# Column sums by TensorE for the weights' scales, and products with the values three ticks behind the scores, in an attention, Fourier and feed-forward kernel

## The chip, the cores and the metric

The kernel runs on one core of one Trainium2 chip. The metric is the device time of one execution in microseconds (us), taken as the median of several executions. Of the kernel before there are three: 1055.57, 1049.64 and 1053.56 us, so the median is 1053.56 us. One more execution was taken with the hardware profiler; it took 1049.91 us.

## The reference

```
q, k, v: (4, 8, 768, 64) float32; centroids: (8, 16, 64); w_ch1: (512, 2048); w_ch2: (2048, 512)

q_assign = argmax(q_n . c_n)            # every query and key goes to one of 16 clusters
k_assign = argmax(k_n . c_n)
mask = q_assign[:, :, :, None] == k_assign[:, :, None, :]
scores = where(mask, q @ k.T / 8, -1e9)
attn = softmax(scores)
x = (attn @ v), heads side by side      # (4, 768, 512)

u = x + real(fft over the sequence of fft over the channels of x)
un = (u - mean) / sqrt(var + 1e-6)
out = u + relu(un @ w_ch1) @ w_ch2
```

## The kernel before

**Numbers in two halves.** Nearly every float32 operand is split into a high and a low float16 part, scaled by a power of two, and a product is three matmuls (high x high, high x low, low x high). Such splits are made by ScalarE (high part) and by VectorE or GpSimd (the rest).

**Attention.** The four sequences have four pairs of heads each, so there are 16 pairs, `pr`. A pair has six row tiles of 128 queries, `st`. One tile is one *tick*: `Attention.scores` (L309) makes the scores of both heads j in PSUM (L320, the mask's product L325), VectorE scales them and takes the extreme of each row in one instruction (L339, output `ju`, row value `m`), ScalarE takes the exponential (L343 in the first sequence, L345 later) and casts it to float16 (L353), GpSimd takes the rest (L354), and a DMA on SyncE's queue transposes both halves into a buffer `pt` (L356). `pt` has `PT` = 5 buffers. `Attention.attend` (L363) multiplies the transposed weights with the values (L374 to L376) into `ps_o`, of which there is one; after every third tile `finish` (L386 to L390, VectorE) divides by the sums and writes X. In the first sequence `ju` is a part of X[1], which is free by then, and the exponential reads it from there, with scale -1; in the later ones `ju` is a bfloat16 scratch tile that nobody reads, and the exponential reads the scores in PSUM with the scale from a column `e`. `prep` brings in a pair: loads, row maxima (L216, L248), scales (L225 to L227), splits (L235, L236), the assignment to clusters (L263 to L303); `split_v` (L199 to L201) splits the values into one of four buffers.

**Weights.** `Weights.run` (L546) brings in the two weight matrices as 32 blocks k of 128 x 512, in steps that lie beside the first sequence's ticks (about 1.46 steps a tick, from the first tick on). float32 values arrive as four 16-bit words each. `largest` (L486) takes the largest absolute value of each row of a block (L491, VectorE) three steps ahead; `signs` (L514) turns the top words into positive and negative parts, two ScalarE instructions a block (L519, L520) one step ahead; `join` (L523) puts them together by two matmuls (L528) and an OR by VectorE (L532); `halve` (L534), one step later, makes the float16 parts with the scale (ScalarE L538, L541, then VectorE L544 or GpSimd L542). The scale is one power of two for each four blocks g of w_ch1, got over the partitions by a matmul and a reduce (`block`, L498, with L48 and L504), and one for each row of w_ch2. `top_power` (L55) makes it by four small VectorE instructions (L58 to L61), on one column for w_ch1 and on four for w_ch2. At the end `relative` (L571) makes the factors that the feed-forward part uses.

**Fourier and feed-forward.** `Fourier.fold` (L647) folds a finished sequence in two and transposes it, `transform` does the DFT by matmuls, `FeedForward.up` (L845) and `down` (L870) are the two products with the weights. They belong to sequence b and run while the attention of sequence b+1 does; those of the last sequence run alone at the end.

**Order of the work.** `Overlap.run` (L981) gives every piece a tick and an order inside it: scores of tick t first (order 1), then the products with the values of tick t - `LAG` (order 3, LAG = 2), splits of values (4.5), weights' steps last (6). TensorE runs its instructions in exactly this order. On the other engines a planner orders them by its own estimate of the times, and each engine then runs its list in order, waiting for semaphores; so does SyncE, which issues all the DMAs. PSUM is 3 buffers `ps_f` of a bank, 2 of `ps_big` for the scores, and the one `ps_o`.

Of the kernel before, what the change touches and what calls it, by code (L numbers as in the profile page):

```python
# [25 lines left out]
P = 128  # L26
# [28 lines left out]
def top_power(nc, tops, s, inv):  # L55

    t = tops.bitcast(I32)
    nc.vector.tensor_scalar(out=t, in0=t, scalar1=20, scalar2=None, op0=ALU.logical_shift_right)  # L58
    nc.vector.tensor_scalar(out=t, in0=t, scalar1=-910.0, scalar2=1.0, op0=ALU.add, op1=ALU.max)
    nc.vector.tensor_scalar(out=inv.bitcast(I32), in0=t, scalar1=240.0, scalar2=float(1 << 23), op0=ALU.min, op1=ALU.mult)  # L60
    nc.vector.reciprocal(out=s, in_=inv)  # L61
# [20 lines left out]
class Attention:  # L82
# [226 lines left out]
    def scores(self, pr, st):  # L309
        nc, sb = self.nc, self.sb  # L310
        assert self.ready >= pr
        (hq, hk), oh, (e, ne) = self.hl[pr], self.oht[pr], self.sc.scores(pr)
# [14 lines left out]
        for j in range(2):  # L327

            m = sb.tile([P, 1], F32, name="rmx", tag="rmx", bufs=6)
            early = pr < H // 2  # L330
            if early:

                n = (2 * st + j) % self.RING * S
                p32 = self.X[1].rearrange("p a x -> p (a x)")[:, n:n + S]
            else:
                p32 = sb.tile([P, S], F32, name="p32", tag="p32", bufs=2)
            x = p32.rearrange("p (h x) -> p h x", h=2)
            ju = x if early else sb.tile([P, 2, SH], BF16, name="ju", tag="ju")
            self.mark = nc.vector.tensor_scalar(out=ju, in0=ps[j][:, :, 0:SH], scalar1=ne, scalar2=None, op0=ALU.mult, op1=ALU.min,  # L339
                                    accum_out=m)  # L340
            self.late = m
            if early:
                nc.scalar.activation(p32, p32, AF.Exp, bias=m, scale=-1.0)  # L343
            else:
                nc.scalar.activation(x, ps[j][:, :, 0:SH], AF.Exp, bias=m, scale=e)  # L345
# [8 lines left out]
            nc.gpsimd.tensor_tensor(out=ph[:, 1], in0=p32, in1=ph[:, 0], op=ALU.subtract)  # L354
# [79 lines left out]
class Weights:  # L434
# [7 lines left out]
    RAW, PN = tuple(4128 * i for i in range(6)) + (29696, 33824), (24768, 26816)  # L442
    ID, TOP, MX = 28864, 29376, 29472
    X32 = 37952, 40000
    EXTRA, A2, AHEAD = 0, 9, 7

    def __init__(self, tc, pool, arena, psf, w1, w2, ident):
# [6 lines left out]
        self.inv = [pool.tile([P, n], F32, name=f"winv{n}") for n in (4, 16)]  # L454
# [31 lines left out]
    def largest(self, k):  # L486

        nc, at = self.nc, self.arena.at
        g, i = divmod(k, 4)
        mx = at(self.MX + 32 * (g % 2), [P, 4], F32)  # L490
        nc.vector.tensor_reduce(out=mx[:, i:i + 1], in_=self.top(k).bitcast(BF16), op=ALU.max, axis=AX.X,  # L491
                                apply_absolute_value=True)
        if i == 3 and g >= 4:
            self.scales(g, mx)
        elif i == 3:
            nc.vector.tensor_reduce(out=mx[:, 0:1], in_=mx, op=ALU.max, axis=AX.X)

    def block(self, g):  # L498

        nc, at = self.nc, self.arena.at  # L500
        mx = at(self.MX + 32 * (g % 2), [P, 4], F32)
        ps = self.psf()
        along(nc, ps[:, 0:P], mx[:, 0:1], self.ident)
        nc.vector.tensor_reduce(out=mx[:, 1:2], in_=ps[:, 0:P], op=ALU.max, axis=AX.X)  # L504
        self.scales(g, mx[:, 1:2])

    def scales(self, g, mx):
        n = mx.shape[1]
        s = self.sb.tile([P, 4], F32, name="wsc", tag="wsc", bufs=2)
        top_power(self.nc, mx, s[:, 0:n], self.inv[0][:, g:g + 1] if n == 1 else self.inv[1][:, 4 * (g - 4):4 * (g - 3)])  # L510
        for i in range(4):
            self.scale[4 * g + i] = s[:, i % n:i % n + 1]

    def signs(self, k):  # L514

        nc, at = self.nc, self.arena.at
        pn = at(self.PN[k % 2], [P, 2, DM], BF16)
        top = self.top(k)
        nc.scalar.activation(pn[:, 0].bitcast(I16), top.bitcast(I16), AF.Relu, bias=self.off[:, 0:1], scale=8.0)  # L519
        nc.scalar.activation(pn[:, 1].bitcast(I16), top, AF.Relu, bias=self.off[:, 1:2], scale=8.0)  # L520
        self.bits[k] = pn
# [12 lines left out]
    def halve(self, k):  # L534
# [4 lines left out]
        if k % 2:  # L539
            x = self.arena.at(self.X32[k // 2 % 2], [P, DM], F32)  # L540
# [5 lines left out]
    def run(self):  # L546
# [5 lines left out]
        for i in range(2):  # L552
            nc.gpsimd.tensor_scalar(out=self.idb[:, i], in0=self.ident, scalar1=1.0 - 2 * i, scalar2=None, op0=ALU.mult)
        for k in range(-self.AHEAD, 33):
# [16 lines left out]
    def relative(self):  # L571

        nc, at = self.nc, self.arena.at
        top, m1, r = (at(self.TOP + 32 * j, [P, 1], F32) for j in range(3))
        rel = self.rel
        nc.vector.tensor_tensor(out=rel.rearrange("p (a c) -> p a c", c=4),
                                in0=self.inv[1].rearrange("p (a c) -> p a c", c=4),
                                in1=self.inv[0].rearrange("p (a o) -> p a o", o=1).broadcast_to([P, 4, 4]), op=ALU.mult)
        nc.vector.tensor_reduce(out=m1, in_=rel, op=ALU.max, axis=AX.X)
        ps = self.psf()  # L580
        along(nc, ps[:, 0:P], m1, self.ident)
        nc.vector.tensor_reduce(out=top, in_=ps[:, 0:P], op=ALU.max, axis=AX.X)
        nc.vector.reciprocal(out=r, in_=top)
        nc.vector.tensor_scalar(out=rel, in0=rel, scalar1=r[:, 0:1], scalar2=HSC, op0=ALU.mult, op1=ALU.mult)
# [36 lines left out]
class Fourier:  # L621
# [25 lines left out]
    def fold(self, b):  # L647
# [5 lines left out]
        mid = at(self.XM, [1, M + 1], F32)  # L653
        nc.gpsimd.tensor_copy(out=mid, in_=X[0:1, 3, 0:M + 1])
        nc.gpsimd.tensor_tensor(out=mid[:, 1:M], in0=mid[:, 1:M], in1=X[0:1, 3, DM - 1:M:-1], op=ALU.add)
        last = at(self.XL, [P, 3], F32)
        xt = {}
        for i, op in self.FOLDS:
# [9 lines left out]
            xt[i] = t.rearrange("p (a t c) x -> p a t c x", a=2, t=3)  # L668
        self.parts[b] = xt, last, mid, s
# [119 lines left out]
HSC = float(2.0 ** -20)  # L789


class FeedForward:


    NT = 2 * P
# [49 lines left out]
    def up(self, blk):  # L845
# [6 lines left out]
        for f in range(16):  # L852
# [9 lines left out]
            if f % 2:  # L862
                nc.vector.tensor_scalar(out=r, in0=ps, scalar1=rel[:, f:f + 1], scalar2=0.0, op0=ALU.mult, op1=ALU.max)  # L863
            else:
                nc.scalar.activation(r, ps, AF.Relu, scale=rel[:, f:f + 1])
            nc.scalar.activation(hh[:, f], ps, AF.Relu, scale=rel[:, f:f + 1])  # L866
# [31 lines left out]
PT = 5  # L898


class Overlap:
# [23 lines left out]
    PIN, PF, PV = (), 29, 1  # L925
    CE, WP, WQ = 0.45, 0, 0
# [54 lines left out]
    def run(self):  # L981
# [43 lines left out]
        for pr in range(NP):  # L1025
# [36 lines left out]
def cluster_attention_fourier_ffn_kernel(ctx, tc, q, k, v, cent, w1, w2, cd, sd, cm, cs, ss, ny, out):  # L1062
# [6 lines left out]
    arena = Arena(glob, 47264)  # L1069
# [47 lines left out]
```

## Time and profile before

| | |
|---|---|
| median of three executions | 1053.56 us (1049.64 to 1055.57) |
| profiled execution | 1049.91 us |
| its span, first to last instruction | 1048.1 us |
| busy: TensorE, VectorE, ScalarE, GpSimd | 910.8, 627.4, 625.3, 586.9 us |
| share of 16 DMA engines, hardware queue | 65.9% |

In the profile PE is TensorE's matmuls, PEld its weight loads, DVE VectorE, ACT ScalarE, POOL GpSimd, SP and SPq SyncE and its queue. A row of a group has line, engine, operation, output and inputs with shapes, the count after the x, then the busy time in us and the mean duration of one in ns, then the idle time of the engine just before and what ended it. A row of waits has who waited for whom, the total in us, how often, and the longest. A row of a window has its bounds, its length, the busy time of each engine with its instructions in brackets, TensorE's granted clock as a share of full speed, the mean busy share of the 16 DMA engines and GB/s. By the start of VectorE's L339 the first sequence's ticks run from 31 to 208 us, those of the second from 208 to 419, of the third from 419 to 643, and of the fourth to 862.

### The profile page before, as it was taken

How to read it: one execution, taken by the hardware profiler on the slowest of the kernel's cores; microseconds unless marked ns; L12 is line 12 of the kernel's file. 1: busy time of each engine (PE TensorE's matmuls, PEld its weight loads, DVE VectorE, ACT ScalarE, POOL GpSimd, SP SyncE). 2: the span in 40 equal slices, each digit the busy share in tenths (PEclk: the TensorE clock that was granted, in tenths of full speed). 3: DMA queues.
4: the chain of work that ended last, by engine and by line, in shares of the span. 5: the costliest groups of instructions: out<-in, count | busy, mean ns of one | idle time of the engine just before them, and what ended most of it. 6: DMA issues, size and time to landing. Idle time of an engine off the chain costs nothing.

```text
span 1048.1 us, 23542 instructions
## 1 busy us (share of the span) xinstructions
PE 910.8 (87%) x9350; PEld 591.7 (56%) x9362; DVE 627.4 (60%) x1297; ACT 625.3 (60%) x980; POOL 586.9 (56%) x693
## 2 busy tenths in 40 slices
PE   3665565749899999998899999997999999999998
PEld 2333333425575756655666757555757667576674
DVE  8789899767757555668656555667555333631110
ACT  4798889755766665645666746556756543351230
POOL 2364565753975756655856646647847645271230
PEclk9987878769899999999899999998999999999999
DMA  7799998979887776568877767588757562321000
GB/s 272 179 225 245 196 239 166 171 156 153 177 123 153 128 154 121 121 137 161 153 137 142 140 128 132 110 141 170 124 102 133 96 110 43 81 52 31 11 11 21
DMA packets 396239, 140.01 MB, mean 134 GB/s; under 512 B 381784, under 2 KB 381792, under 8 KB 396128
## 3 DMA queue, kind: packets, MB, share of 16 engines
q1 hardware_dynamic: 396128, 138.50, 65.9%
q8 instruction: 73, 1.20, 0.5%
q14 instruction: 38, 0.31, 0.1%
HBM read 42.52 MB, written 6.29 MB: 47 GB/s over the span
## 4 chain that ended last, share of the span: by engine, by line
PE 39%; DVE 6%; DMA 3%; ACT 3%; POOL 2%; issue 2%; SPq 0%; ACTq 0%; DVEq 0%; POOLq 0%
PE ps_f L888 16%; PE ps_f L858 13%; PE ps_big L320 3%; DMA pt<-ph 3%; PE ps_f L713 2%; DVE ju L339 1%; ACT p L345 1%; PE ps_o L374 1%; POOL ph L354 1%; PE ps_o L375 1%; PE ps_o L376 1%; PE ps_big L325 1%; ACT ph L353 1%; DMA scr<-in_k_dram 0%; DVE arena L660 0%
## 5 line engine op out<-in xcount | busy, mean ns | idle before, releaser
L354 POOL TENSOR_TENSOR ph<-p,ph 128x768 f16<-128x768 f32 x144 | 242.9, 1688 | 184.6 <-ACT ph L353 150.1
L858 PE MATMUL ps_f<-arena,w1h 128*128 128x256 f16 x1536 | 271.4, 277 | 19.1 <-ACT arena L866 9.0
L888 PE MATMUL ps_f<-w2h,arena 128*128 128x512 f16 x768 | 238.9, 379 | 0.0
L345 ACT ACTIVATE p<-ps_big,rmx,sce 128x768 f32<-128x768 f32 x144 | 142.1, 988 | 132.9 <-DVE ju L339 127.5
L858 PE MATMUL ps_f<-arena,w1l 128*128 128x256 f16 x768 | 212.4, 277 | 0.0
L339 DVE TENSOR_SCALAR_CACHE_REDUCE ju<-ps_big,sce 128x768 bf16<-128x768 f32 x144 | 146.1, 1014 | 68.2 <-PE ps_big L325 58.2
L888 PEld LDWEIGHTS <-arena 128*128 128x128 f16 x1152 | 108.7, 98 | 126.6 <-issue 5.2
L858 PEld LDWEIGHTS <-w1h 128*128 128x128 f16 x1536 | 152.1, 99 | 36.0 <-issue 14.3
L867 POOL TENSOR_TENSOR arena<-arena 128x256 f16<-128x256 f32 x192 | 128.1, 677 | 77.3 <-ACT arena L866 73.6
L320 PE MATMUL ps_big<-hlk,hlq 64*128 64x384 f16 x1152 | 128.9, 348 | 39.0 <-ACT p L345 23.4
L374 PE MATMUL ps_o<-v,pt 128*128 128x66 f16 x1152 | 124.8, 198 | 43.0 <-DVE X L390 27.5
L888 PE MATMUL ps_f<-w2l,arena 128*128 128x512 f16 x384 | 145.5, 379 | 0.0
L374 PEld LDWEIGHTS <-pt 128*128 128x128 f16 x1152 | 110.2, 100 | 57.7 <-issue 37.1
L353 ACT CAST ph<-p 128x768 f16<-128x768 f32 x144 | 119.6, 832 | 15.0 <-DMA pt<-ph 12.8
L375 PE MATMUL ps_o<-v,pt 128*128 128x64 f16 x1152 | 124.8, 199 | 0.0
L376 PE MATMUL ps_o<-v,pt 128*128 128x66 f16 x1152 | 124.5, 198 | 0.0
L866 ACT ACTIVATE arena<-ps_f,wrel 128x256 f16<-128x256 f32 x192 | 90.1, 472 | 54.8 <-DVE arena L863 54.7
L863 DVE TENSOR_SCALAR arena<-ps_f,wrel 128x256 f32<-128x256 f32 x96 | 46.3, 482 | 124.9 <-PE ps_f L858 66.4
L320 PEld LDWEIGHTS <-hlq 64*128 64x128 f16 x1152 | 55.5, 99 | 101.5 <-issue 72.7
L375 PEld LDWEIGHTS <-pt 128*128 128x128 f16 x1152 | 110.7, 101 | 2.8
L376 PEld LDWEIGHTS <-pt 128*128 128x128 f16 x1152 | 111.1, 103 | 0.0
L858 PEld LDWEIGHTS <-w1l 128*128 128x128 f16 x768 | 76.1, 99 | 20.2 <-issue 10.7
(178 smaller groups left out, 1330.4 us busy)
## 6 DMA issues: line engine op xcount, KB each, us to landing
arena<-in_moe_w_ch_dram SPq DMA_DIRECT2D x32, 512.0 KB, 6.8
scr<-in_q_dram SPq DMA_DIRECT2D x16, 384.0 KB, 2.9
scr<-in_k_dram SPq DMA_DIRECT2D x16, 384.0 KB, 4.5
vst<-in_v_dram SPq DMA_DIRECT2D x16, 384.0 KB, 3.5
out_dram<-arena SPq DMA_DIRECT2D x24, 256.0 KB, 2.3
pt<-ph SPq DMA_TRANSPOSE x168, 3.9
arena<-in_cs_dram SPq DMA_DIRECT2D x12, 192.0 KB, 3.5
arena<-in_ss_dram SPq DMA_DIRECT2D x12, 192.0 KB, 3.5
```

The source lines that it names most:

```text
L320: nc.tensor.matmul(out=ps[j][:, hf, 0:SH], lhsT=hq[rows[j], a, sl], rhs=hk[rows[j], c, hs], start=(i == 0), stop=False)
L339: self.mark = nc.vector.tensor_scalar(out=ju, in0=ps[j][:, :, 0:SH], scalar1=ne, scalar2=None, op0=ALU.mult, op1=ALU.min, accum_out=m)
L345: nc.scalar.activation(x, ps[j][:, :, 0:SH], AF.Exp, bias=m, scale=e)
L353: nc.scalar.copy(out=ph[:, 0], in_=p32)
L354: nc.gpsimd.tensor_tensor(out=ph[:, 1], in0=p32, in1=ph[:, 0], op=ALU.subtract)
L374: nc.tensor.matmul(out=o[:, at:at + W], lhsT=hi, rhs=v16[:, kt, 0:W], start=(kt == 0), stop=False)
L375: nc.tensor.matmul(out=o[:, at:at + D], lhsT=hi, rhs=v16[:, kt, 66:130], start=False, stop=False)
L376: nc.tensor.matmul(out=o[:, at:at + W], lhsT=lo, rhs=v16[:, kt, 0:W], start=False, stop=(kt == ST - 1))
L858: nc.tensor.matmul(out=ps.rearrange("p (t x) -> p t x", x=P), lhsT=a[:, dc, fs], rhs=c[:, :, dc], start=(i == 0), stop=(i == 11))
L866: nc.scalar.activation(hh[:, f], ps, AF.Relu, scale=rel[:, f:f + 1])
L867: nc.gpsimd.tensor_tensor(out=hl[:, f], in0=r, in1=hh[:, f], op=ALU.subtract)
L888: nc.tensor.matmul(out=ps, lhsT=a[:, f, ts], rhs=c[:, f], start=(i == 0), stop=(i == 47))
```

## The change

The row maxima (`largest`, L491) go. Instead the new `block` multiplies, for four blocks of weights, the positive and negative parts (`bits`) by a matrix of ones on TensorE: eight matmuls into one bank give the sums over the 128 rows for each of 512 columns, on every partition; one VectorE reduce takes the largest, and `top_power` works on that one column, for both matrices. `signs` treats two blocks in one pair of instructions, two steps ahead, into three buffers instead of two. `join` is as before, but comes after `block` in the step. In the first sequence the products with the values come three ticks after the scores, up to the 22nd tile; `pt` has six buffers in all sequences. In the later sequences `ju` lies in PSUM over the scores, and the exponential reads it there with the constant scale -1. The copies for the middle row of the Fourier part (`mid`, two small GpSimd instructions) are moved behind the two folds. `x` in `halve` has one buffer instead of two, some places and constants change with it, and `relative` needs no matmul.

```diff
-def top_power(nc, tops, s, inv):
+def top_power(nc, tops, t, s, inv):
-    t = tops.bitcast(I32)
-    nc.vector.tensor_scalar(out=t, in0=t, scalar1=20, scalar2=None, op0=ALU.logical_shift_right)
-    nc.vector.tensor_scalar(out=t, in0=t, scalar1=-910.0, scalar2=1.0, op0=ALU.add, op1=ALU.max)
+    t = t.bitcast(I32)
+    nc.vector.tensor_scalar(out=t, in0=tops.bitcast(I32), scalar1=23, scalar2=None, op0=ALU.logical_shift_right)
+    nc.vector.tensor_scalar(out=t, in0=t, scalar1=-13.0, scalar2=1.0, op0=ALU.add, op1=ALU.max)
...
-            ju = x if early else sb.tile([P, 2, SH], BF16, name="ju", tag="ju")
+            ju = x if early else ps[j][:, :, 0:SH]
...
-            if early:
-                nc.scalar.activation(p32, p32, AF.Exp, bias=m, scale=-1.0)
-            else:
-                nc.scalar.activation(x, ps[j][:, :, 0:SH], AF.Exp, bias=m, scale=e)
+            nc.scalar.activation(x, ju, AF.Exp, bias=m, scale=-1.0)
...
+    def block(self, g):
+        nc, at = self.nc, self.arena.at
+        ps = self.psf()
+        i = 0
+        for k in range(4 * g, 4 * g + 4):
+            for j in range(2):
+                nc.tensor.matmul(out=ps, lhsT=self.ones[:, 0:1].broadcast_to([P, P]), rhs=self.bits[k][:, j], start=(i == 0), stop=(i == 7))
+                i += 1
+        mx = at(self.MX + 32 * (g % 2), [P, 1], F32)
+        nc.vector.tensor_reduce(out=mx, in_=ps, op=ALU.max, axis=AX.X)
+        s = self.sb.tile([P, 1], F32, name="wsc", tag="wsc", bufs=2)
+        top_power(nc, mx, ps[:, 0:1], s, self.inv[g // 4][:, g % 4:g % 4 + 1])
+        for i in range(4):
+            self.scale[4 * g + i] = s[:, 0:1]
...
     def signs(self, k):
-        pn = at(self.PN[k % 2], [P, 2, DM], BF16)
-        top = self.top(k)
+        pn = at(self.PN[k // 2 % 3], [P, 2, 2, DM], BF16)
+        raw = at(self.RAW[k % len(self.RAW)], [P, 2, 4 * DM + 16], U16)
+        top = raw[:, :, 4:4 + 4 * DM].rearrange("p a (n f) -> p a n f", f=4)[:, :, :, 0]
         nc.scalar.activation(pn[:, 0].bitcast(I16), top.bitcast(I16), AF.Relu, bias=self.off[:, 0:1], scale=8.0)
         nc.scalar.activation(pn[:, 1].bitcast(I16), top, AF.Relu, bias=self.off[:, 1:2], scale=8.0)
-        self.bits[k] = pn
+        self.bits[k], self.bits[k + 1] = pn[:, :, 0], pn[:, :, 1]
...
         for k in range(-self.AHEAD, 33):
-            if k >= 1 and k % 4 == 1 and k < 16:
-                self.block(k // 4)
             for p in self.loads(k):
                 self.load(p)
-            if 0 <= k + 3 < 32:
-                self.largest(k + 3)
-            if 0 <= k + 1 < 32:
-                self.signs(k + 1)
+            if k % 2 == 0 and 0 <= k + 2 < 32:
+                self.signs(k + 2)
+            if k % 4 == 0 and 0 <= k < 32:
+                self.block(k // 4)
             if 0 <= k < 32:
                 self.join(k)
             if k >= 1:
                 self.halve(k - 1)
...
-PT = 5
+PT = 6
...
+    LATE = 22
...
                 at(t0 + st, 1, att.scores, pr, st)
-                at(t0 + st + self.LAG, 3, att.attend, pr, st)
+                at(t0 + st + self.LAG + (6 * pr + st < self.LATE), 3, att.attend, pr, st)
```

More of the change, by code (lines that the diff above doesn't have):

```diff
@@ L452, in __init__ @@
         self.dsc = pool.tile([P, 1], F32, name="dsc")
-        self.inv = [pool.tile([P, n], F32, name=f"winv{n}") for n in (4, 16)]
+        self.inv = [pool.tile([P, 4], F32, name=f"winv{n}") for n in range(2)]
         self.rel = pool.tile([P, 16], F32, name="wrel")
@@ L861, in up @@
             r = at(self.HR[f % 2], [P, self.NT], F32)
[L862 to L866, printed above, removed]
+            with self.tc.high_priority() if self.HP else contextlib.nullcontext():
+                if f % 2:
+                    nc.vector.tensor_scalar(out=r, in0=ps, scalar1=rel[:, f:f + 1], scalar2=0.0, op0=ALU.mult, op1=ALU.max)
+                else:
+                    nc.scalar.activation(r, ps, AF.Relu, scale=rel[:, f:f + 1])
+                nc.scalar.activation(hh[:, f], ps, AF.Relu, scale=rel[:, f:f + 1])
             nc.gpsimd.tensor_tensor(out=hl[:, f], in0=r, in1=hh[:, f], op=ALU.subtract)
```

60 lines of the change are left out of this document (20 added, 40 removed).

## The prediction

> **What bounds the kernel now.** I read the table of windows first, cut at the ticks of each sequence, because a share of the whole span would mix stages that have different limits.
>
> ```profile
> core 0: us, PE busy (x) PEld busy (x) DVE busy (x) ACT busy (x) POOL busy (x), PEclk, DMA share, GB/s
> 0.00:31.00 31.00, 12.95 (x52) 6.60 (x53) 25.04 (x72) 15.15 (x24) 5.54 (x38) 1.00 0.68 239
> 31.00:208.00 177.00, 110.58 (x1313) 65.58 (x1324) 151.08 (x311) 153.17 (x219) 105.02 (x90) 0.83 0.96 207
> 419.00:643.00 224.00, 211.56 (x2313) 139.26 (x2311) 142.73 (x287) 137.48 (x215) 139.55 (x162) 0.98 0.72 137
> 643.00:862.00 219.00, 207.22 (x2263) 136.35 (x2262) 126.20 (x255) 131.46 (x203) 134.36 (x152) 0.98 0.70 127
> ```
>
> From 419 us on TensorE is busy for 94 to 95% of the time and is the limit. In the first sequence, 31 to 208 us, it is busy for 62%; VectorE is at 85%, ScalarE at 87%, and the DMA share reads 0.96. So in the stage that the weights share with the first sequence there are three candidates, and the change works on two of them. Next I asked what ScalarE and TensorE waited for in that window.
>
> ```profile
> ACT X L343 <- DVE X L339: 7.6, 5, 2.5
> ACT w2h L538 <- DVE ps_f L532: 5.8, 6, 2.7
> ACT w1h L538 <- DVE wsc L61: 4.6, 3, 3.0
> ...
> PE ps_o L374 <- DVE X L390: 27.5, 6, 5.5
> PE ps_big L320 <- DVE X L339: 14.8, 17, 3.7
> PE ps_o L374 <- DMA pt<-p: 8.2, 7, 2.6
> PE ps_o L374 <- DMA pt<-ph: 6.8, 4, 2.2
> PE ps_f L528 <- DVE w1l L544: 4.6, 3, 2.8
> ```
>
> ScalarE is idle for 177 - 153.2 = 23.8 us, and 18.0 us of it is waiting for VectorE. TensorE waits 42.3 us for VectorE and 15.0 us for transposes that have not landed. VectorE runs late, and the others queue behind it. Last I looked at the DMA share in short windows, to see what 0.96 means.
>
> ```profile
> 78.00:80.00 2.00, 2.00 (x39) 1.31 (x39) 2.00 (x3) 2.00 (x4) 0.00 (x0) 1.00 1.00 399
> 94.00:100.00 6.00, 3.90 (x57) 2.37 (x57) 5.21 (x11) 2.83 (x5) 3.07 (x2) 0.88 1.15 204
> 121.00:122.00 1.00, 0.66 (x19) 0.66 (x20) 0.90 (x4) 0.87 (x2) 0.00 (x0) 1.00 0.00 0
> ```
>
> With loads alone, 399 GB/s, a full microsecond reads 1.00; with transposes, 204 GB/s, it reads 1.15, since packets overlap; and there are gaps of 0.00. So 0.96 over 177 us is 148 us (at 1.15) to 170 us (at 1.00) of full use. The change moves the same bytes, so this is a floor under the stage.
>
> **The scales, on VectorE.** The rows by form:
>
> ```profile
> L491 DVE TENSOR_REDUCE arena<-arena 128x1 f32<-128x512 bf16 x32 | 21.7, 680 | 8.0 <-DMA arena<-in_moe_w_ch_dram 7.9
> L504 DVE TENSOR_REDUCE arena<-ps_f 128x1 f32<-128x128 f32 x4 | 1.1, 284 | 0.6 <-PE ps_f L48 0.6
> L59 DVE TENSOR_SCALAR arena<-arena 128x4 int32<-128x4 int32 x4 | 4.6, 1143 | 0.1
> L60 DVE TENSOR_SCALAR winv<-arena 128x4 int32<-128x4 int32 x4 | 6.2, 1547 | 0.1
> L60 DVE TENSOR_SCALAR winv<-arena 128x1 int32<-128x1 int32 x4 | 0.6, 151 | 0.1
> L277 DVE TENSOR_REDUCE mx<-ps_f 128x24 f32<-128x384 f32 x16 | 8.8, 551 | 0.6 <-PE ps_f L271 0.6
> L216 DVE TENSOR_REDUCE amx<-scr 128x1 f32<-128x768 f32 x32 | 30.4, 950 | 22.4 <-DMA scr<-in_q_dram 19.4 <-DMA scr<-in_k_dram 2.8
> ```
>
> Removed: 32 row maxima, 21.7 us; four L504, 1.1; the four-column chain of w_ch2, 4.6 + 6.2 for L59 and L60 and 8 x 0.151 = 1.2 for its other two, costed as one-column ones; the one-column chain of w_ch1, 16 x 0.151 = 2.4. Together 37.2 us. Added: eight reduces of 512 columns from PSUM. The slope from L277 to L216 is (950 - 551) / 384 = 1.04 ns a column, so one costs 551 + 128 x 1.04 = 684 ns, eight 5.5 us; and 32 one-column instructions, 4.8 us. Together 10.3 us, net 26.9 us less.
>
> Not all of it lies in the stage; eight maxima run ahead of it, of which these are the first and the last:
>
> ```profile
> 9.28 0.68 DVE L491 TENSOR_REDUCE arena<-arena 128x1 f32<-128x512 bf16 x1
> ...
> 21.59 0.68 DVE L491 TENSOR_REDUCE arena<-arena 128x1 f32<-128x512 bf16 x1
> ```
>
> So the stage loses 24 x 0.68 + 15.5 = 31.8 us and gains seven eighths of 10.3, 9.0 us: VectorE there goes from 151.1 to about 128 us. Ahead of the stage VectorE is busy for 25 of 31 us, with the first pair's preparation between those maxima. But eight of the new matmuls now stand ahead of the first scores. I take 1 us off, between 3 us off (most maxima had delayed that preparation) and 3 us on (the matmuls are late).
>
> **The signs, on ScalarE, and the sums, on TensorE.**
>
> ```profile
> L519 ACT ACTIVATE arena<-arena 128x512 int16<-128x512 int16 x32 | 24.1, 753 | 4.6 <-PE ps_f L528 1.6 <-PE ps_o L376 1.5 <-DMA scr<-in_q_dram 1.5
> L520 ACT ACTIVATE arena<-arena 128x512 int16<-128x512 uint16 x32 | 24.0, 749 | 0.0
> L199 ACT ACTIVATE v<-vst,scp 128x384 f16<-128x384 f32 x32 | 18.4, 611 | 0.0
> L235 ACT ACTIVATE hlk<-scr,scp 128x768 f16<-128x768 f32 x16 | 14.7, 921 | 0.0
> L528 PE MATMUL ps_f<-arena 128*128 128x512 bf16 x52 | 22.0, 510 | 6.8 <-DVE w1l L544 4.6 <-DVE arena L58 1.0 <-issue 0.7
> ```
>
> From L199 to L235 a further element costs (921 - 611) / 384 = 0.81 ns. A sign instruction of 1024 elements is then 0.75 + 512 x 0.81 = 1.17 us; 32 of them 37.3 us in place of 48.1. I put 9.7 us of these 10.8 in the stage: ScalarE goes from 153.2 to 143.5 us. TensorE gets 64 matmuls of L528's form, 22.0 / 52 = 0.42 us each, 27 us in all: in the stage from 111 to about 135 of some 165 us. It has that room; what hides the matmuls is its present waiting.
>
> What the change adds is an order. `block` stands in TensorE's list ahead of `join` and the next scores, and it needs signs issued in the same step, where `join` had its signs a step earlier. If ScalarE is late with them, `join`, the next tick's scores, and so VectorE's L339 and ScalarE's own next exponential stand behind. Bounds: 0 if the planner places the signs early, as now, where L528 waits for VectorE and ScalarE is not in its list; and 8 x (2 x 1.17 + 8 x 0.42) = 46 us if signs and matmuls are exposed every time. I take 0.3 us a group, 2.4 us, near the lower end because of that list. The wait of L538 for the scale, 4.6 us with four groups, now comes with eight: another 4.6 us.
>
> **Sum of the stage.** ScalarE is the engine that I count by: its work 143.5, its idle time 23.8, of which I take off half of the 18.0 us of waits for VectorE, because VectorE's share falls from 85% to 128 / 165 = 78% and not to zero; and the new 2.4 + 4.6. That gives 143.5 + 23.8 - 9.0 + 7.0 = 165.3 us in place of 177, or 11.7 less. It lies in the middle of the DMA floor of 148 to 170.
>
> **Three ticks and six buffers.** These can take away the 15.0 us in which TensorE waits for transposes, or nothing: the longer wait of the same L374, 27.5 us for L390, stays, because there is still one `ps_o` and VectorE releases it. With six buffers and three ticks all six are in use when tile t is transposed, so its DMA needs the products of tile t - 3, which TensorE runs just before; if they are late, the loads behind it on SyncE's queue wait too. And the values' buffers come free a tick later:
>
> ```profile
> POOL v L200 <- PE ps_o L376: 16.5, 4, 7.1
> POOL w1l L542 <- ACT arena L541: 12.8, 5, 4.3
> ```
>
> GpSimd already stands for 16.5 us before L200, with L354 and so the transposes behind it. One tick more (177 / 24 = 7.4 us) at each of four places is 30 us of GpSimd at worst, of which it has 177 - 105 = 72 idle. Gain and loss face each other; I take 0, between 15 off and 15 on. The single buffer of `x` costs nothing, because L542 waits for ScalarE and not the other way round; the moved GpSimd copies and the shorter `relative` are costed at nothing as well, and the fold would show it if they delayed it.
>
> **`ju` in PSUM, in the later sequences.**
>
> ```profile
> L339 DVE TENSOR_SCALAR_CACHE_REDUCE ju<-ps_big,sce 128x768 bf16<-128x768 f32 x144 | 146.1, 1014 | 68.2 <-PE ps_big L325 58.2 <-ACT arena L866 2.0 <-DVE ju L339 0.9
> L227 DVE TENSOR_REDUCE ps_f<-ps_f 128x3 f32<-128x384 f32 x16 | 8.9, 559 | 15.1 <-PE ps_f L48 15.1
> L345 ACT ACTIVATE p<-ps_big,rmx,sce 128x768 f32<-128x768 f32 x144 | 142.1, 988 | 132.9 <-DVE ju L339 127.5 <-POOL ph L354 5.4
> L641 ACT ACTIVATE arena<-ps_f 128x257 f16<-128x257 f32 x24 | 9.3, 388 | 15.6 <-PE ps_f L728 9.8 <-PE ps_f L713 4.1 <-DVE arena L642 1.1
> L866 ACT ACTIVATE arena<-ps_f,wrel 128x256 f16<-128x256 f32 x192 | 90.1, 472 | 54.8 <-DVE arena L863 54.7
> PE ps_big L320 <- ACT p L345: 10.1, 8, 3.0
> ```
>
> A reduce into PSUM (L227) costs 8 ns more than one into SBUF (L277), so L339 goes to about 1022 ns. An activation from PSUM with a constant scale (L641) costs 84 ns less than one with the scale from a column (L866), so L345 goes to about 904 ns: 12.1 us less of ScalarE. It is on the path only where TensorE waits for it: after 250 us, 10.1 us in eight stretches (last row). Two exponentials a tick make 0.17 us off each, 1.3 us, and VectorE gives some of it back: 1 us off, between 12 off and 2 on.
>
> [...]
>
> **Total.** 1 + 11.7 + 0 + 1 = 13.7 us off the profiled 1049.9 gives 1036.2 us. The median of the runs lies 3.7 us above that profiled execution, so I forecast 1040 us.
>
> **Rivals.** The first is that the loop closes up. If all of ScalarE's waits for VectorE go and no new ones come, the stage is 143.5 + 5.8 = 149 us, at the lower DMA floor; with the other 2 us that is 30 off, 1024 us. For it: VectorE would be at 86% there only if nothing else slowed it. Against it: DMA would have to run without the gaps shown.
>
> The second is that DMA is already the limit, and the lag does nothing because six buffers just cover three ticks. At the upper floor of 170 us with gaps as today, the stage saves 2 us, and the total is 1050 us. For it: 0.96. Against it: the window at 0.00, and SyncE's transposes wait for GpSimd's results.
>
> The third is slower: TensorE stuck in `block`, waiting for signs that ScalarE has placed behind exponentials. If half of the 46 us is exposed, 23 us against 13.7 give 1063 us. From 1.7 us a group on it eats the gain; from 2.4 us the kernel is slower by half a per cent. For it: ScalarE is 87% busy and in order. Against it: the signs depend on loads made long before.
>
> **Chances.** A measurement of this kernel can tell about 0.5%, 5.3 us, from no change. The forecast case has 0.58, the loop closing up 0.12, DMA 0.16, the stuck list 0.14. The first two are faster, the third is about no change, the fourth slower. The range takes in the loop closing up, DMA, and the bounds of the small terms: 1024 to 1056 us.
>
> **What would show it.** In the profile after: no L491; eight reduces of 128x512 near 0.68 us; signs near 1.17 us; ticks 0 to 24 of L339 in about 165 us with VectorE near 128 and ScalarE near 143.5; L345's successor near 0.90 us; few waits of the products for `pt`. I am wrong if the first stage has not become shorter, if the column sums wait for ScalarE by more than 1.7 us a group, or if later stages move by more than 5 us.

## The result, and the profile after

The changed kernel takes 1042.51 us (median of 7 runs, 1041.02 to 1048.06); beside it the kernel before took 1051.6 us (7 runs, the three already shown among them). The ratio is 0.9914 with a 95% interval of 0.9893 to 0.9935: about 9 us faster, which is more than the 0.5% that a measurement can tell. The profiled execution after took 1042.51 us with a span of 1040.7; the one before, 1049.91, lies at the low end of its runs, so the two spans differ by only 7.4 us.

Where did those 7.4 us come from? I cut both spans at the starts of L339 in ticks 0, 24, 48, 72 and 95. A sequence has 24 ticks, so these are the prefix, the four sequences and the tail (us):

| part | before | after | difference |
|---|---|---|---|
| ahead of the first L339 | 31.1 | 28.8 | -2.3 |
| ticks 0 to 24, first sequence with the weights | 177.4 | 162.7 | -14.7 |
| ticks 24 to 48 | 210.5 | 217.4 | +6.9 |
| ticks 48 to 72 | 223.8 | 224.6 | +0.8 |
| ticks 72 to 95 | 213.6 | 214.2 | +0.6 |
| from tick 95 to the end | 191.7 | 193.0 | +1.3 |

The first two rows give 17.0 us, and the later parts take 9.6 back, 6.9 of it in ticks 24 to 48; each of the last three differs by about 1 us, which single profiles can't tell from nothing. The windows of the kernel after, cut at the same places, with busy time of each engine, granted clock, DMA share and GB/s:

```profile
core 0: us, PE busy (x) PEld busy (x) DVE busy (x) ACT busy (x) POOL busy (x), PEclk, DMA share, GB/s
...
28.80:191.50 162.70, 114.63 (x1336) 64.83 (x1356) 136.41 (x285) 143.07 (x187) 102.74 (x89) 0.83 1.00 222
191.50:408.90 217.40, 188.46 (x2137) 124.66 (x2134) 136.38 (x282) 127.84 (x202) 139.89 (x153) 0.94 0.74 143
408.90:633.50 224.60, 211.80 (x2310) 138.97 (x2309) 140.68 (x286) 132.77 (x215) 140.40 (x162) 0.98 0.73 138
```

In the first sequence (28.80 to 191.50) VectorE has 14.7 us less to do than before and ScalarE 10.1, and the stage is shorter by 14.7. The DMA share now reads 1.00 at 222 GB/s, with the same bytes in less time. What the engines waited for in that window (total us, times, longest):

```profile
PE ps_big L320 <- DVE X L339: 13.4, 18, 2.9
PE ps_o L371 <- DVE X L387: 7.4, 1, 7.4
PE ps_o L371 <- DMA pt<-p: 4.8, 5, 2.1
PE ps_f L515 <- ACT arena L528: 4.0, 2, 2.7
...
ACT X L342 <- DVE X L339: 9.8, 7, 5.5
...
ACT w1h L525 <- DVE wsc L61: 2.0, 1, 2.0
ACT w2h L525 <- DVE ps_f L519: 1.4, 2, 1.1
```

L371 is the old L374, the products with the values. Its waits for VectorE (27.5 us before) are one of 7.4 us, and those for transposes of `p` and `ph` (15.0) have mostly gone. The groups of the kernel after that answer to the rows priced:

```profile
L494 DVE TENSOR_REDUCE arena<-ps_f 128x1 f32<-128x512 f32 x8 | 5.4, 681 | 0.8 <-PE ps_f L491 0.8
L60 DVE TENSOR_SCALAR winv<-ps_f 128x1 int32<-128x1 int32 x8 | 1.2, 155 | 0.1
L506 ACT ACTIVATE arena<-arena 128x1024 int16<-128x1024 int16 x16 | 19.6, 1222 | 4.9 <-PE ps_f L491 3.3 <-DMA arena<-in_moe_w_ch_dram 1.6
L507 ACT ACTIVATE arena<-arena 128x1024 int16<-128x1024 uint16 x16 | 19.4, 1210 | 0.0
L491 PE MATMUL ps_f<-arena 128*128 128x512 bf16 x60 | 17.5, 430 | 2.1 <-DVE w1l L531 1.6 <-issue 0.2
L339 DVE TENSOR_SCALAR_CACHE_REDUCE ps_big<-ps_big,sce 128x768 f32<-128x768 f32 x144 | 141.4, 1020 | 44.2 <-PE ps_big L325 44.2
L339 DVE DVE_READ_ACCUMULATOR ps_big<-ps_big,sce 128x1 f32 x144 | 20.3, 141 | 0.0
L342 ACT ACTIVATE p<-ps_big,rmx 128x768 f32<-128x768 f32 x144 | 128.9, 900 | 133.8 <-DVE ps_big L339 120.3 <-POOL ph L351 5.9 <-POOL rpow L825 3.3
```

The row maxima (the old L491) are gone; L491 is now the column sums' matmul, which waits for no signs (VectorE's L531 leads its short wait).

### The profile page after: what moved, and what is told of

The parts are those of the page before. It is cut to its first block, busy times and chain, and to the rows that moved or that the text cites. A ratio compares the mean times of both kernels' runs of the same rounds, so it can differ in the third digit from the quotient of the medians.

```text
span 1040.7 us, 23567 instructions
## 1 busy us (share of the span) xinstructions
PE 916.0 (88%) x9396; PEld 592.0 (57%) x9416; DVE 607.9 (58%) x1264; ACT 604.3 (58%) x948; POOL 588.1 (57%) x694
## 4 chain that ended last, share of the span: by engine, by line
PE 43%; DVE 14%; DMA 9%; POOL 9%; ACT 7%; issue 7%; SPq 1%; ACTq 0%; POOLq 0%; DVEq 0%
PE ps_f L873 17%; PE ps_f L842 15%; PE ps_big L320 4%; DMA pt<-ph 4%; POOL ph L351 3%; DVE ps_big L339 3%; ACT ph L350 2%; DMA scr<-in_k_dram 2%; DMA arena<-arena 1%; PE ps_o L371 1%; ACT p L342 1%; PE ps_f L697 1%; PE ps_o L372 1%; PE ps_o L373 1%; DVE X L339 1%
## 5 line engine op out<-in xcount | busy, mean ns | idle before, releaser
L351 POOL TENSOR_TENSOR ph<-p,ph 128x768 f16<-128x768 f32 x144 | 241.8, 1687 | 181.3 <-ACT ph L350 149.0
L842 PE MATMUL ps_f<-arena,w1l 128*128 128x256 f16 x768 | 211.9, 276 | 0.0
L342 ACT ACTIVATE p<-ps_big,rmx 128x768 f32<-128x768 f32 x144 | 128.9, 900 | 133.8 <-DVE ps_big L339 120.3
L842 PEld LDWEIGHTS <-w1h 128*128 128x128 f16 x1536 | 151.9, 99 | 36.7 <-issue 12.7
L339 DVE TENSOR_SCALAR_CACHE_REDUCE ps_big<-ps_big,sce 128x768 f32<-128x768 f32 x144 | 141.4, 1020 | 44.2 <-PE ps_big L325 44.2
L320 PE MATMUL ps_big<-hlk,hlq 64*128 64x384 f16 x1152 | 127.7, 346 | 36.2 <-ACT p L342 22.1
L371 PE MATMUL ps_o<-v,pt 128*128 128x66 f16 x1152 | 121.8, 197 | 14.5 <-DVE X L387 7.4
L848 DVE TENSOR_SCALAR arena<-ps_f,wrel 128x256 f32<-128x256 f32 x96 | 46.2, 481 | 136.4 <-POOL arena L852 82.1
L371 PEld LDWEIGHTS <-pt 128*128 128x128 f16 x1152 | 108.6, 99 | 27.6 <-issue 16.8
L372 PE MATMUL ps_o<-v,pt 128*128 128x64 f16 x1152 | 121.7, 197 | 0.0
L373 PE MATMUL ps_o<-v,pt 128*128 128x66 f16 x1152 | 121.2, 196 | 0.0
L372 PEld LDWEIGHTS <-pt 128*128 128x128 f16 x1152 | 109.2, 99 | 2.7
L373 PEld LDWEIGHTS <-pt 128*128 128x128 f16 x1152 | 109.4, 101 | 0.0
```

The costliest lines, as they stand in the source:

```text
L320: nc.tensor.matmul(out=ps[j][:, hf, 0:SH], lhsT=hq[rows[j], a, sl], rhs=hk[rows[j], c, hs], start=(i == 0), stop=False)
L342: nc.scalar.activation(x, ju, AF.Exp, bias=m, scale=-1.0)
L371: nc.tensor.matmul(out=o[:, at:at + W], lhsT=hi, rhs=v16[:, kt, 0:W], start=(kt == 0), stop=False)
L372: nc.tensor.matmul(out=o[:, at:at + D], lhsT=hi, rhs=v16[:, kt, 66:130], start=False, stop=False)
L373: nc.tensor.matmul(out=o[:, at:at + W], lhsT=lo, rhs=v16[:, kt, 0:W], start=False, stop=(kt == ST - 1))
L842: nc.tensor.matmul(out=ps.rearrange("p (t x) -> p t x", x=P), lhsT=a[:, dc, fs], rhs=c[:, :, dc], start=(i == 0), stop=(i == 11))
```

## The experiments

Two questions were open: which part of the change the stage's 14.7 us come from, since I had priced the third tick at nothing; and why the later sequences lost time. Ratios are against the kernel before, run on the same chip; the stage is ticks 0 to 24 in one profiled execution of each. Four kernels whose first sequence is computed nearly alike (the kernel before, `ju` alone, `ju` in turns and the `mid` copies alone) gave 177.4, 176.5, 178.3 and 176.1, so a difference of 2 us there says nothing. Each stage below is read from one profile.

**Only the weights' part.** The scales from column sums and the signs in pairs stay; two ticks, five buffers, the old `ju` and the old place of the `mid` copies come back. On the changed kernel:

```diff
...
-PT = 6
+PT = 5
...
-                at(t0 + st + self.LAG + (6 * pr + st < self.LATE), 3, att.attend, pr, st)
+                at(t0 + st + self.LAG, 3, att.attend, pr, st)
```

> The kernel before with the weights' part of the change alone: column sums on TensorE, signs in pairs, shorter relative; lag 2, five buffers, ju and the middle row as before. Theory A (the load of VectorE and ScalarE in the first sequence is what was shortened): ticks 0 to 24, 177.4 us before and 162.7 after the whole change, come to 163 to 168 us, and the time falls by 6 to 12 us. Theory B (three ticks and six buffers did it, by taking away TensorE's waits): ticks 0 to 24 stay at 173 to 178 us and the time falls by under 4 us. Of the 6.9 us that the second sequence lost, this run shows them again only if the weights' part or its shift causes them.

Measured: 1054.33 us, 1.0038 (1.0018 to 1.0057), so no gain, rather a small loss. Its stage, and what TensorE waited for in it:

```profile
28.20:209.00 180.80, 122.34 (x1379) 66.53 (x1379) 128.51 (x286) 145.95 (x189) 106.59 (x90) 0.80 0.95 205
```

```profile
PE ps_o L374 <- DMA pt<-p: 26.9, 12, 7.0
PE ps_o L374 <- DMA pt<-ph: 9.7, 6, 3.9
PE ps_big L320 <- DVE X L339: 8.7, 10, 1.9
PE ps_o L374 <- DVE X L390: 5.4, 1, 5.4
```

VectorE does have the 128.5 us that I had forecast, 22.6 less than before, and yet the stage lasts 180.8. TensorE's waits have moved: 14.1 us for VectorE in these rows where L390 and L339 alone were 42.3, but 36.6 for transposes where it was 15.0. The theory that VectorE's load alone was the limit falls.

**Only the three ticks, the six buffers and `ju`.** On the kernel before:

```diff
...
-PT = 5
+PT = 6
...
+    LATE = 22
...
-                at(t0 + st + self.LAG, 3, att.attend, pr, st)
+                at(t0 + st + self.LAG + (6 * pr + st < self.LATE), 3, att.attend, pr, st)
```

> The kernel before with the lag of three ticks, six buffers and ju in PSUM, but with the row maxima and the scales as before (six buffers leave no room for ju in SBUF, so the two go together). Theory A: ticks 0 to 24 stay within 4 us of 177.4, the time within 4 us of before. Theory B: ticks 0 to 24 fall to 163 to 168 us, the time by 6 to 12 us. Beside the run with ju alone it gives the lag and the buffers by difference.

Measured: 1057.09 us, 1.0057 (1.004 to 1.0074), stage 177.0. `ju` alone, shown further down, takes 1057.02 us, so the third tick and the sixth buffer add nothing to it. TensorE's waits in it:

```profile
PE ps_big L320 <- DVE X L339: 31.1, 26, 3.5
PE ps_f L525 <- DVE w1l L541: 8.9, 3, 3.8
PE ps_f L525 <- DVE w2l L541: 4.8, 1, 4.8
PE ps_o L371 <- DMA pt<-p: 4.4, 2, 3.0
...
PE ps_o L371 <- DMA pt<-ph: 2.4, 1, 2.4
```

This is the mirror image. The transposes cost 6.8 us, and VectorE 44.8 in the rows shown. So the theory that the pipeline's depth alone was the limit falls too.

**The whole change with two ticks.** If each part takes away one of two limits that stand close behind one another, then taking the third tick out of the whole change must lose the stage's gain:

```diff
-    LATE = 22
+    LATE = 0
```

> The whole change, but with the products two ticks behind the scores everywhere (LATE = 0); six buffers stay. The parts alone had shown that the sums without the lag only move TensorE's waits, from VectorE's L390 to the transposes. Theory C (the two parts need each other: the sums take the load off VectorE, the third tick hides the path from scores to transposed weights): ticks 0 to 24 go back from 162.7 to 175 us or more, TensorE's waits of the products for pt to 25 us or more, the time to 1052 us or more. Theory D (six buffers, or a lucky order of the lists, made the change faster): ticks 0 to 24 stay under 168 us, the time under 1046 us.

Measured: 1061.96 us, 1.0084 (1.0046 to 1.0121), stage 180.4. TensorE waits for transposes again, 35.0 us:

```profile
PE ps_o L371 <- DMA pt<-p: 27.8, 12, 5.9
PE ps_big L320 <- DVE X L339: 10.2, 12, 1.6
PE ps_o L371 <- DMA pt<-ph: 7.2, 6, 1.7
```

The stage in all four combinations:

| us, ticks 0 to 24 | old scales | column sums |
|---|---|---|
| two ticks behind | 177.4 | 180.4 and 180.8 |
| three ticks behind | 177.0 | 162.7 |

In this stage neither part is worth anything alone, and together they are worth 14.7 us. (Both kernels with three ticks, and the one of 180.4 us, also have `ju` in PSUM and six buffers. In the first sequence `ju` is as before, and the last experiment shows what the sixth buffer is worth.)

**Row maxima back on VectorE.** Is it VectorE's relief, or ScalarE's, that makes the difference once there are three ticks? Here the 32 row maxima are computed in addition, and nothing uses them:

```diff
+            if 0 <= k + 3 < 32:
+                nc.vector.tensor_reduce(out=at(29600, [P, 4], F32)[:, k % 4:k % 4 + 1], in_=self.top(k + 3).bitcast(BF16), op=ALU.max,
+                                        axis=AX.X, apply_absolute_value=True)
```

> The whole change, and the 32 row maxima put back on VectorE beside it, their results unused: 21.8 us of VectorE again, everything else as in the whole change. Theory C with VectorE as the engine that was relieved: ticks 0 to 24 go from 162.8 to 170 us or more, TensorE's waits for VectorE grow by 10 us or more. If ScalarE's shorter signs or the smaller chains did it: under 166 us.

Measured: 1066.3 us, 1.0136 (1.0101 to 1.0172). The prefix is 37.2 us in place of 28.8, and the stage 179.2. What ScalarE waited for in that stage begins with

```profile
ACT X L342 <- DVE X L339: 26.0, 10, 5.6
```

where the whole change had 9.8. All of TensorE's waits for VectorE together go from 33.2 to 44.7 us. ScalarE's own work is the same, but the gain of the stage is gone:

```profile
37.20:216.40 179.20, 119.97 (x1336) 67.61 (x1355) 144.46 (x306) 142.64 (x185) 103.88 (x89) 0.79 0.92 202
L547 DVE TENSOR_REDUCE arena<-arena 128x1 f32<-128x512 bf16 x23 | 15.6, 683 | 12.6 <-DMA arena<-in_moe_w_ch_dram 12.6
```

So the gain hangs on the row maxima being off VectorE's list. Their work is only one part of that. VectorE is busy for 144.5 us in place of 136.4, 8.1 more, and the stage is 16.5 longer: in its list VectorE also stands for 12.6 us before maxima whose blocks have not landed. In the kernel before that row has 7.9 us of such idle time, which I had not counted. How much of the gain is the work and how much these waits was not separated.

**Signs one block at a time.** The counterpart for ScalarE: on the changed kernel, four sign instructions of 512 columns in place of two of 1024.

```diff
-        nc.scalar.activation(pn[:, 0].bitcast(I16), top.bitcast(I16), AF.Relu, bias=self.off[:, 0:1], scale=8.0)
-        nc.scalar.activation(pn[:, 1].bitcast(I16), top, AF.Relu, bias=self.off[:, 1:2], scale=8.0)
+        for j in range(2):
+            nc.scalar.activation(pn[:, 0, j].bitcast(I16), top[:, j].bitcast(I16), AF.Relu, bias=self.off[:, 0:1], scale=8.0)
+            nc.scalar.activation(pn[:, 1, j].bitcast(I16), top[:, j], AF.Relu, bias=self.off[:, 1:2], scale=8.0)
```

> The whole change with the signs of a pair of blocks made by four ScalarE instructions of 512 elements in place of two of 1024, about 9 to 11 us more of ScalarE in ticks 0 to 24. If ScalarE's work is on the path there, as the prediction counted it: 162.8 goes to 170 us or more. If it is covered: within 3 us.

Measured: 1042.91 us, 0.9909 (0.9877 to 0.994), the same as the changed kernel. In its stage,

```profile
27.40:191.30 163.90, 112.39 (x1325) 62.61 (x1344) 133.11 (x287) 149.44 (x215) 104.22 (x90) 0.86 1.00 223
```

ScalarE is busy 6.4 us longer than in the changed kernel (149.4 to 143.1) and the stage only 1.2 us. So much of ScalarE's shorter signs is covered.

**Eight loads fewer.** The DMA share of 1.00 could mean that the transfers are now the limit. This kernel leaves out 8 of the 32 loads of the weights: for every second block of the second matrix it computes with what lay in the buffer.

```diff
-                self.load(p)
+                if p < 16 or p % 2 == 0:
+                    self.load(p)
```

> The whole change with eight of the 32 loads of weights left out (every second block of the second matrix keeps what lay in the buffer), about 8 x 1.6 = 13 us less of DMA in ticks 0 to 24, with all else unchanged. If DMA is what limits this stage now (its share reads 1.00): ticks 0 to 24 fall from 162.8 to 150 to 156 us. If it is only busy beside the others: 160 to 163 us.

Measured: 1040.57 us, 0.9907 (0.9875 to 0.9939); stage:

```profile
30.60:195.00 164.40, 112.12 (x1323) 64.65 (x1342) 133.39 (x285) 144.31 (x188) 104.31 (x90) 0.84 0.96 195
```

The rate falls from 222 to 195 GB/s and the stage does not become shorter. The amount of data moved is not the limit of this stage.

**Only `ju` in PSUM.** Now the later sequences. On the kernel before:

```diff
-            ju = x if early else sb.tile([P, 2, SH], BF16, name="ju", tag="ju")
+            ju = x if early else ps[j][:, :, 0:SH]
...
-                nc.scalar.activation(x, ps[j][:, :, 0:SH], AF.Exp, bias=m, scale=e)
+            nc.scalar.activation(x, ju, AF.Exp, bias=m, scale=-1.0)
```

> The kernel before with ju in PSUM and the constant scale alone. By the prediction's term: L345's successor at 0.90 us, L339 at 1.02 us, the time 1 us less, between 12 less and 2 more. If the new form is what costs the second sequence its 6.9 us, ticks 24 to 48 go from 210.5 to about 217 us and the time is 4 to 7 us more.

Measured: 1057.02 us, 1.0056 (1.0036 to 1.0076): a loss of 5.9 us, although each exponential is shorter (a mean of 900 ns in place of 988). The reason stands in ScalarE's list. One tick of the third sequence in the kernel before (start, duration, instruction):

```profile
616.72 0.99 ACT L345 ACTIVATE p<-ps_big,rmx,sce 128x768 f32<-128x768 f32 x1 [3.07 <-DVE ju L339]
617.75 0.83 ACT L353 CAST ph<-p 128x768 f16<-128x768 f32 x1
618.49 0.99 ACT L345 ACTIVATE p<-ps_big,rmx,sce 128x768 f32<-128x768 f32 x1
619.50 0.83 ACT L353 CAST ph<-p 128x768 f16<-128x768 f32 x1
```

and the same tick with `ju` alone changed:

```profile
620.14 1.84 ACT L342 ACTIVATE p<-ps_big,rmx 128x768 f32<-128x768 f32 x2 [1.56 <-DVE ps_big L339]
622.45 0.83 ACT L350 CAST ph<-p 128x768 f16<-128x768 f32 x1 [0.47 <-DMA pt<-ph]
624.24 0.83 ACT L350 CAST ph<-p 128x768 f16<-128x768 f32 x1 [0.96 <-DMA pt<-ph]
```

Exponential, cast, exponential, cast has become exponential, exponential, cast, cast. This tick is no exception: of the 72 ticks of the later sequences, 65 have a cast between the two exponentials in the kernel before, and 7 with `ju` alone. The first head's cast, and with it GpSimd's L351 and the transpose, starts 2.31 us after the tick's first exponential where it was 1.03; only 0.47 of that is a wait for its buffer. The changed kernel has the new order as well, with a cast between in 7 of 72 ticks.

**`ju` in PSUM, the heads in turns.** The kernel before with the last edit, and the second head's exponential held behind the first head's cast:

```diff
-            nc.scalar.activation(x, ju, AF.Exp, bias=m, scale=-1.0)
+            with self.tc.issue_after(cast.ins) if j and not early else contextlib.nullcontext():
+                nc.scalar.activation(x, ju, AF.Exp, bias=m, scale=-1.0)
...
-                nc.scalar.copy(out=ph[:, 0], in_=p32)
+                cast = nc.scalar.copy(out=ph[:, 0], in_=p32)
```

> The kernel before with ju in PSUM alone, as in the run of ju alone, and in the later sequences the second head's exponential is put behind the first head's cast, as ScalarE's list had it before; ju in PSUM had made the list exponential, exponential, cast, cast. Theory E (the list's new order is what made ju alone slower, by 0.56%, because the first head's cast, rest and transpose start an exponential later): the time comes back to within 2 us of before, and by the 84 ns less of the exponential perhaps 1 us under it. Theory F (the PSUM form itself costs it: VectorE's write, or the two engines in one bank): it stays 4 us or more above before.

Measured: 1045.55 us, 0.9935 (0.9913 to 0.9957). The same data in the same places, with the order alone changed, goes from a loss of 5.9 us to a gain of 6.5. The order was the cause of the loss. (Of the gain, a part may come from the 7 ticks that were not in turns in the kernel before; that was not separated. Its profiled execution, 1050.31 us, lies near the top of its runs of 1042.01 to 1050.9, so its parts aren't compared here.)

**The whole change, the heads in turns.** The same two lines on the changed kernel.

> The whole change, with the same order of exponentials and casts in the later sequences. Theory E: ticks 24 to 48 go from 217.3 to about 213 us, the rest loses about 2 us, and the time falls from 1042.5 to 1036 to 1040 us. Theory F: no change from 1042.5.

Measured: 1036.21 us, 0.9846 (0.982 to 0.9871), where the change has 1042.51 us and 0.9914: 6 to 7 us faster than the change and the best version here. One tick of it:

```profile
618.96 0.90 ACT L343 ACTIVATE p<-ps_big,rmx 128x768 f32<-128x768 f32 x1 [6.60 <-DVE ps_big L339]
619.89 0.83 ACT L351 CAST ph<-p 128x768 f16<-128x768 f32 x1
620.63 0.89 ACT L343 ACTIVATE p<-ps_big,rmx 128x768 f32<-128x768 f32 x1
621.55 0.83 ACT L351 CAST ph<-p 128x768 f16<-128x768 f32 x1
```

Ticks 48 to 72 take 222.2 us (224.6 in the changed kernel), 72 to 95 211.0 (214.2), the tail 190.4 (193.0). But ticks 24 to 48 stay at 218.5, so what they lost has another cause.

**The `mid` copies.** Moved behind the folds on the kernel before, and back ahead of them on the changed kernel; the edit of the second is

```diff
+        mid = at(self.XM, [1, M + 1], F32)
+        nc.gpsimd.tensor_copy(out=mid, in_=X[0:1, 3, 0:M + 1])
+        nc.gpsimd.tensor_tensor(out=mid[:, 1:M], in0=mid[:, 1:M], in1=X[0:1, 3, DM - 1:M:-1], op=ALU.add)
...
-        mid = at(self.XM, [1, M + 1], F32)
-        nc.gpsimd.tensor_copy(out=mid, in_=X[0:1, 3, 0:M + 1])
-        nc.gpsimd.tensor_tensor(out=mid[:, 1:M], in0=mid[:, 1:M], in1=X[0:1, 3, DM - 1:M:-1], op=ALU.add)
```

> The kernel before with the middle row's two GpSimd copies behind the folds, alone. By the prediction nothing: within 2 us. If GpSimd's list in the fold is what costs the second sequence, ticks 24 to 48 go from 210.5 to 215 us or more, and the third and fourth sequences lose as well.

> The whole change, with the middle row's two GpSimd copies ahead of the folds as before. Alone they had cost 0.17% (0.02 to 0.32). If that holds beside the other parts: 1 to 3 us less than 1042.5, most of it in ticks 24 to 48; if it was the planner's list and no more, within 2 us either way.

Measured: 1053.39 us, 1.0017 (1.0002 to 1.0032), and 1045.09 us, 0.9932 (0.9906 to 0.9957). The first interval leaves out 1 only just, and the second overlaps that of the change (0.9893 to 0.9935); its ticks 24 to 48 take 216.5 us. If the place of the copies costs anything, it is under the 0.5% that can be told.

**Five buffers.** The best version with

```diff
-PT = 6
+PT = 5
```

> The whole change with exponentials and casts in turns (1036.2 us), but with five buffers pt in place of six; the lag stays at three ticks. If the sixth buffer is needed for the third tick (with five, a transpose must wait for products two ticks sooner in TensorE's list): ticks 0 to 24 go from 162.5 to 168 us or more, and SyncE's transposes wait for TensorE's products. If the lag alone does it: within 2 us. If six buffers are what costs the second sequence (218.5 us against 210.1 without the other parts), ticks 24 to 48 fall by 4 us or more.

Measured: 1036.41 us, 0.9858 (0.9828 to 0.9888), stage 164.1 (162.4 with six), ticks 24 to 48 218.8. The sixth buffer brings nothing measurable: it is the third tick that counts.

## Why the prediction was right, and where its steps failed

The time came out at 1042.5 for 1040, inside the range, and faster as forecast. The working behind it was only partly right, and that the total is near is in part luck: 13.7 us off were forecast and 9.1 measured, but in the profiles the prefix and the stage gave 17.0 where I had 12.7, and the later sequences took 9.6 where I had 1 off.

**Prefix.** 1 us off was forecast, 2.3 measured. With the maxima back beside the column sums the prefix is 37.2 us, so maxima there do delay the first pair's preparation, as the gaining bound had it. The size is not told well: the kernels with column sums and without maxima have 27.4 to 30.6 us.

**The prices.** Those of single instructions held: the reduce of 512 columns 681 ns (684 forecast), L339's main part 1020 (1022), the exponential 900 (904). The signs take 1222 and 1210 ns, 4 to 5% above the 1166 worked out, and ScalarE in the stage 143.1 us (143.5). The sums on TensorE I had priced too high: L491 is busy for 17.5 us in its 60 recorded matmuls where I had 27 for 64, and TensorE has 114.6 us in the stage where I said 135. VectorE has 136.4 where I said 128. Most of that is no part of the change: the 12 instructions that build `oh`, L289 and L293, take 3.4 + 8.1 us in place of 2.1 + 3.0, 6.4 more. Their place in time has changed: see below. The same waiting stood in a row that I took off. L59 and L60 on four columns have means of 1143 and 1547 ns in the kernel before. Seven of the eight are long (1327 to 1606 ns) and end within 0.1 us of a GpSimd pass of L354; the eighth, L59 at 163.63 us, takes 0.15. So of the 10.8 us of these two rows most was waiting, and not work of the scales.

**Sum of the stage, counted by ScalarE.** It gave 165.3 us and 162.7 came, but the step failed. Lengthening ScalarE's signs by 6.4 us moved the stage by 1.2, while the maxima on VectorE alone took the whole gain away. ScalarE's 9.7 us were not what was saved; the size came out near because what I took off for its work and half of its waits happened to sum to what the loop gained. The terms for `block` and for the scale, 7.0 us together, were also too much: L491 doesn't wait for the signs, and the two waits of L525 shown are 3.4 us where the four groups had 10.4 in two rows of the same kind.

**"Three ticks and six buffers": "I take 0".** This is the step that was most wrong. Under the new scales the third tick is worth 180.4 - 162.7 = 17.7 us, beyond the 15 off that I had as its bound; under the old scales 0.4. The loss that I had set against its gain did not come: GpSimd's wait for the values' buffers, 16.5 us before, became

```profile
POOL v L200 <- PE ps_o L373: 1.7, 1, 1.7
```

I had added up terms that hang on each other: I booked 9.0 us of relief from VectorE without asking what stands next, and the 15.0 us of waits for transposes stood next. In the first experiment they grew to 36.6. The sixth buffer is worth nothing measurable, with or against me.

**`ju` in PSUM: "1 us off".** Alone it costs 5.9 us, outside my bounds of 12 off to 2 on, because of the order in which ScalarE's list came out, which I had not considered. With the order held it gains 6.5, between my bounds; why it is that and not 1 was not read. What VectorE gives back was priced too low too, at 8 ns an instruction from rows with small outputs. L339's main part does grow by only 6 ns, 1014 to 1020. But in the kernel before, the read of its accumulator was

```profile
L339 DVE DVE_READ_ACCUMULATOR ju<-ps_big,sce 128x1 f32 x144 | 11.9, 83 | 0.0
```

and after it is 141 ns. Together that is 64 ns an instruction, 9.2 us over 144, where 8 ns had made 1.2; 58 of the 64 ns stand in a record of their own. They did not keep the kernel before with `ju` in turns from being faster (0.9935).

**Later sequences.** I had said that I would be wrong if they moved by more than 5 us. They moved by 9.6. What the third, the fourth and the tail lost is about 1 us each; in turns all three fall below the kernel before. Ticks 24 to 48, +6.9, stay unexplained. In the kernel before they are

```profile
208.50:419.00 210.50, 188.03 (x2109) 123.28 (x2110) 135.48 (x280) 131.50 (x201) 136.38 (x153) 0.93 0.78 146
```

TensorE's work is the same after, 188.5 us, and no single wait has grown by the 6.9: all of TensorE's waits there go from 22.1 to 28.9 us, those for ScalarE from 19.4 to 22.1, for transfers from 1.4 to 4.4, for VectorE from 1.3 to 2.4. It is not the lag (217.6 without it), the place of the `mid` copies (216.5), the sixth buffer (218.8) or the order of the exponentials (218.5). The column sums alone gave 211.9 and `ju` alone 214.0, and the lag with `ju` 215.2; every kernel with both the sums and `ju` in PSUM has 216 or more. That a first sequence that ends sooner leaves other work to the second fits the three-tick kernels, but not the one with two ticks, whose stage is long and which still has 217.6. I leave it open.

**Rivals.** The loop did not close up: 149 us of stage were not reached, with VectorE at 136.4 / 162.7 = 84%. DMA as the limit falls with the eight loads fewer. Its floor of 170 us was none: the stage took 162.7, and with the same bytes the share times the length fell with it, from 0.96 x 177 = 170 to 1.00 x 162.7. (The 2 us that I gave this rival in the stage don't follow from that floor, which would leave 7.) The list stuck in `block` isn't seen: L491 waits for no signs. What TensorE does wait for is the end of `block`'s chain, VectorE's L60, which still uses the bank of the sums: 6.4 us in three waits of other lines (L263, L515, L48). ScalarE's next signs waited 3.3 us once for L491.

## What to carry to other kernels

Two limits that stand close behind one another in a loop, here what stands in one engine's list and the depth at which the next stage follows, give nothing when one of them is removed (stages of 180.8 and 177.0 us for 177.4) and much when both are (162.7): when a wait is to go, price the next one in the same table and ask whether it merely grows. After any edit, read the order in which an in-order engine's list has come out, for a changed dependence can reorder it, and that was worth 12 us here (1.0056 and 0.9935 of the time before). And test each part both alone and taken out of the whole, since either half of that would have misled here.

## What the runs showed of the hardware

The VectorE instruction of 128x768 with an accumulated output (L339) paid here for a PSUM destination in the separate read of its accumulator, 83 ns before and 141 after (140 with `ju` alone), and hardly in its own record, 1014 and 1020. It is not the float32 type: in the first sequence after, where the output is float32 in SBUF, the read takes 81 ns.

Some small VectorE instructions lasted much longer beside a GpSimd pass. The rows of `oh` after, in the window of the first sequence,

```profile
L293 DVE TENSOR_TENSOR oh<-ac,mx 128x96 bf16<-128x96 f32 x8 | 8.1, 1045 | 0.0
L289 DVE TENSOR_TENSOR oh<-ac,mx 128x192 bf16<-128x192 f32 x4 | 3.4, 839 | 0.1
```

and before,

```profile
L293 DVE TENSOR_TENSOR oh<-ac,mx 128x96 bf16<-128x96 f32 x8 | 3.0, 411 | 0.0
L289 DVE TENSOR_TENSOR oh<-ac,mx 128x192 bf16<-128x192 f32 x4 | 2.1, 515 | 0.0
```

differ by 6.4 us. After, the pair of L293 at 98.89 us took 2.01 us, and the first of it, 1.70 us, ended just after GpSimd's L351 of 98.71 to 100.47; before, the pair at 109.06 took 0.42, with GpSimd idle until 109.21. It does not always happen: before, a one-column L59 at 56.44 took 0.15 us although GpSimd's L354 ran from 56.21 to 57.86. What in the two engines makes them wait was not tried.

A DMA share of 1.00 over a whole stage was no limit: with 8 of 32 loads gone it read 0.96, and the stage took 164.4 us where it had taken 162.7.
